# New margins and key offsets in the planner of an attention and mixture-of-experts kernel

## The chip, the cores and the metric

The kernel runs on one core of one Trainium2 chip. The metric is the device time of one execution in microseconds. Three runs of the kernel before gave 558.15, 562.72 and 568.16 us; their median, 562.72 us, is the time that a change is held against.

## The reference, cut to what matters

Linear attention without a softmax feeds a mixture of experts with top-1 routing. The shapes: 8 batches ("blocks" below), 8 heads, 576 rows, 64 columns per head, so 4608 tokens of 512 columns; 8 experts with a hidden width of 1024; a capacity of 1152 tokens per expert. All inputs are fp32.

```python
kv = np.einsum('bhsd,bhse->bhde', k, v)
out = np.einsum('bhsd,bhde->bhse', q, kv)
rms = np.sqrt(np.mean(out * out, axis=-1, keepdims=True) + 1e-06)
x = (out / rms * g_norm)                      # then (B, H, S, D) -> (B*S, H*D)
...
logits = x @ w_gate
expert_idx = np.argmax(logits, axis=1)        # gate_w: its softmax probability
...
h = np.maximum(np.einsum('ecd,edf->ecf', disp, w1), 0.0)   # disp: an expert's tokens, in order
y = np.einsum('ecf,efd->ecd', h, w2)
out[i] = gate_w[i] * y[expert_idx[i], pos[i]]
```

## The kernel before

The work has two stages, each with a plan of its own.

**Attention stage** (first plan, some 155 us with the first expert's beginning). For each of the 8 blocks, `load` (L736) fetches k, v and q in halves of four heads. `kv_products` (L758) makes k-transposed times v for each half: one run of 36 products of 64 columns, in TensorE's rows `a<-v_sb,k_sb` and `misc<-v_sb,k_sb` of L772 in turn. These are the "k and v runs". Their sums are copied (`kvs`), transposed (L801), copied again (`kvt`), multiplied with the gate's weights (the gate product, L810) and spread into a block-diagonal right-hand side, `kv_bd`. `unit` (L829) transposes q (L843, four transposes or one), copies (`qt`) and multiplies with `kv_bd` (the attention products, L861, or L864 for half rows) into `o_sb`, which also gets the gate's logits.

`route` (L905) does the top-1 routing of a block, mostly on VectorE: sums of squares (`ss`, L894), the root, logits, the winner's one-hot `ohe`. Then come two products on TensorE, both with key FIRST, the most urgent. `place` (L995, matmuls of L1003, "first routing product") counts each token's position within its expert; VectorE turns the positions into one-hots (`ohl` L1032, `ohh` L1035, `rhs` L1039). `enter` (L1044, matmuls of L1046, "second routing product") adds the tokens to a table. The results, rows with logits, go to DRAM (`x_dram`).

After block 2 the largest expert so far is picked (`early_weights`, L1166): its weights are loaded in quarters into `raw`, VectorE takes maxima of eight pieces (`top`, L361, tile `am`), and a scale follows through two small products (L374, L381) and six short steps of VectorE. After block 4 the first 384 tokens of that expert are gathered (`early_slots` L1208, `rows` L1230: an indirect DMA, a scaling `norm` L465 into `xm`, four transposes L477, the "turning", a high half L713 and a low half L485 of `xs`) and its products begin while the last blocks still run.

**Expert stage** (second plan). For each of 8 experts, products with w1 (L551, three terms of fp16 halves), a ReLU into high and low halves `hb` (L556 on ScalarE, L559 on VectorE), products with w2 (`second`, L1262; L597, or L612 and L627 for narrow tiles), an eviction with a scale (`ysb`, L632 on ScalarE) and a scattering DMA (L637). Weights of the next expert are split (`weights`, L1611) and its rows gathered (`rows_beside`, L1663) beside that.

**What sets the order.** `Plan` (L111) is a list scheduler that runs while the kernel is built. Every `op` has ways (engine and assumed duration), dependences, a key and a margin `late`. An op may start when its dependences have ended, plus a lag between the engines, plus `late` (L145). The planner takes, over all engines, the op that can start soonest; among those of an engine that could start then, the lowest key wins. `NUDGE` holds two tables, one for each plan, that add an offset to the key of single ops by their number. The resulting order is emitted as it is, engine by engine. The margins only steer this order; on the chip nobody waits for a margin.

In the kernel before, the margins are 1.9 us for the second run of a block's k and v products (`KV_APART`, L64 and L778), `LANDED` (3.0) for rows of the later experts, and those of two small products. `place`, `enter`, the maxima and the first gathered rows have none.

```python
return op(("T", KV), go, [ts["k", half][1], ts["v", half][1]] + mm, key + (0, 0.8)[half], banks, (kh, vh),
          late=KV_APART if half and b else 0.0)
```

Of the kernel before, what the change touches and what calls it, by code (L numbers as in the profile page):

```python
# [12 lines left out]
F32 = mybir.dt.float32  # L13
I32 = mybir.dt.int32
AF = mybir.ActivationFunctionType
ALU = mybir.AluOpType
# [5 lines left out]
EARLY_AFTER = 4  # L22
# [24 lines left out]
FIRST = -50.0  # L47
# [25 lines left out]
GATHER = 1.2  # L73
LANDED = 3.0
TURNED_PAIR = {64: 2.7, 48: 2.2, 32: 1.8}
NUDGE = (
# [10 lines left out]

# [102 lines left out]
def attention_moe_kernel(  # L190
# [12 lines left out]
    nc = tc.nc  # L203
    NB, H, S, D = q.shape
    N, DM = out.shape
    E = w_gate.shape[1]
    F = w1.shape[2]
    P = 128
# [225 lines left out]
    def spans(s0, s1):  # L434

        cuts = [s0] + list(range((s0 // P + 1) * P, s1, P)) + [s1]
        return [(a, b - a, NHI if a % P else a // P) for a, b in zip(cuts, cuts[1:])]
# [89 lines left out]
    class Gemm1:  # L527
# [14 lines left out]
        def out(self, t, j):  # L542
            return t[:, j, 0:self.n].rearrange("p (u x) -> p u x", u=self.nh)
# [29 lines left out]
    class Gemm2:  # L573
# [50 lines left out]
        def turn(self, i, yp):  # L624
            n = self.tiles[i][1]
            for dt in range(KD):
                nc.tensor.transpose(yp[0:n, dt * P:(dt + 1) * P], self.yt[:, dt * n:(dt + 1) * n], ident)  # L627

        def out(self, i, yp):
            n = self.tiles[i][1]  # L630
            self.ysb = self.pool.tile([P, DM], F32, tag="ysb", name="ysb", bufs=self.bufs)
            nc.scalar.activation(self.ysb[0:n], yp[0:n, 0:DM], AF.Copy, scale=self.ysc[0:n, i:i + 1])  # L632
            return self.ysb
# [71 lines left out]
    op = plan.op  # L705
# [199 lines left out]
    def route(b, oh, ssh, outs, sums):  # L905
# [99 lines left out]

        bp = op(("T", 0.4), place, [ohe] + accs[-1:] + reads[-1:], FIRST)
        acc = V(0.08, lambda: nc.vector.tensor_tensor(out=tot_acc, in0=tot_acc, in1=z["oh_sum"], op=ALU.add),
# [43 lines left out]
        o2 = V(0.45, low_hot, [lo], takes=(lh,))  # L1051
        ent = op(("T", 0.21), enter, [o, o2] + enters[-1:] + readers.pop("tab", []), FIRST, (), (rh, lh))
        enters.append(ent)
# [112 lines left out]
    def early_weights():  # L1166
# [11 lines left out]
        for i, key in ((0, W1_KEY), (1, W2_KEY)):  # L1178
# [6 lines left out]
            for p in range(4):  # L1185
                key = WKEYS[i][0] + 2 * p * WKEYS[i][1]
                if TOPS[i][p] == "A":
                    tops += [op(("A", 0.8), lambda e, f=f, p=p: f["sum"](p), [loads[p // 2]], key)
                             for p in (2 * p, 2 * p + 1)]
                else:  # L1190
                    tops += [op(("V", 0.61), lambda e, f=f, p=p: f["top"](p), [loads[p // 2]], key)
                             for p in (2 * p, 2 * p + 1)]
# [37 lines left out]
    def rows(gidx, s0, s1, n, slots_, key, low, pool, raw, bank, hold=None, size=None):  # L1230
# [10 lines left out]
        for i in range(len(spans(s0, s1))):  # L1241
# [4 lines left out]
            a = op([("V", 0.61), ("P", 1.05)], lambda e, i=i: st["rows"].norm(i, nc.vector if e == "V" else nc.gpsimd), [o],  # L1246
                   low, (xm,), (xg,), port="VP")
            gates.append(op(("V", 0.07), lambda e, i=i: st["rows"].gate(i), [o], low, (), (xg, hold)))

# [12 lines left out]
    def second(r, st, hh, hl, w2, scaled, hid, w_hold, sl_hold, s0, s1, bank, tiles=range(NHI), key=None):  # L1262
# [3 lines left out]
        for i, (_, m, _) in enumerate(spans(s0, s1)):  # L1266
# [37 lines left out]

            o = op(("A", 0.58), out_, [o], urgent, (yh,), (yp,))
            o = op(("P", 1.05), lambda e, i=i, yh=yh: st["g2"].write(i, yh.t), [o], key, (), (yh, sl_hold))
            o = op(("D", 0.73), None, [o], key, (), (yh,))
# [303 lines left out]
    def weights(r, key, after, after2):  # L1611

        ws, sets, zs, holds = wsets[r % 2], [], [], []
        for i in range(2):
# [19 lines left out]
            for p in range(8):  # L1634
                if MOE_TOPS[i][p] == "A":
                    tops.append(op(("A", 0.8), lambda e, f=f, p=p: f["sum"](p), [loads[p // 2]], key, (hold,),
                                   (raws[p // 2],)))
                else:
                    tops.append(op(("V", 0.61), lambda e, f=f, p=p: f["top"](p), [loads[p // 2]], key, (),
                                   (raws[p // 2],)))  # L1640
            x = new("x")
# [21 lines left out]
    def rows_beside(r, key):  # L1663
# [9 lines left out]
        for i in range(n):  # L1673
            xg, xm, pair = new("xg"), new("xm"), new("pair")

            def fetch(e, i=i):
                if i == 0:
# [9 lines left out]
                   lambda e, i=i: st["x"].norm(i, by_letter[e]), [o], key - 5 if r == 1 else key + 1,  # L1687
                   (xm,), (xg,), late=0.0 if r == 1 else LANDED, port="VP")
            gates.append(op(("P", 0.25), lambda e, i=i: st["x"].gate(i, nc.gpsimd), [a], key + 1, (), (xg, hold)))
# [120 lines left out]
```

## Time and profile before

| | |
|---|---|
| median of three runs | 562.72 us (558.15 to 568.16) |
| profiled execution | 556.98 us, span 555.1 us |
| mean granted clock of TensorE | 0.985 |
| TensorE busy | 520.3 us, 94% of the span |
| VectorE busy | 394.1 us, 71% |
| ScalarE busy | 252.7 us, 46% |
| GpSimd busy | 150.9 us, 27% |

The engines are named PE (TensorE's matmuls), PEld (its weight loads), DVE (VectorE), ACT (ScalarE), POOL (GpSimd) and SP (the queue that issues most loads). Matmuls overlap in a pipeline, so the start of the next row tells more of a matmul's length than its own duration does. "Issue" marks idle time for which the profile shows nothing that was waited for.

### The profile page before, as it was taken

The page shows a single profiled execution, that of the slowest core. Times are in us where ns is not written, and L with a number is a line of the kernel's source. Part 1 is how long each engine was busy: PE and PEld are TensorE (multiplying, and loading weights), DVE is VectorE, ACT ScalarE, POOL GpSimd, SP SyncE. Part 2 cuts the span into 40 slices and gives each one's busy share as a digit, 9 for nine tenths or more (in the row PEclk, how much of TensorE's full clock was granted, in tenths as well). Part 3 has the DMA queues.
Part 4 walks back from the last instruction along what each step waited for, and adds up shares of the span by engine and source line. Part 5 has one row for each costly group of instructions (what it writes and reads, how often), then busy time and mean ns, then how long its engine had stood idle before and what let it go on. Part 6 is the DMA issues. An engine that isn't in the chain of part 4 may idle for free.

```text
span 555.1 us, 12017 instructions
## 1 busy us (share of the span) xinstructions
PE 520.3 (94%) x4599; PEld 344.2 (62%) x4599; DVE 394.1 (71%) x1041; ACT 252.7 (46%) x506; POOL 150.9 (27%) x173
## 2 busy tenths in 40 slices
PE   4989797898996999999999999999999999999995
PEld 4878695876544666546754675667468648745442
DVE  3389679989967679869868899779778785751200
ACT  1667475698413346237246282264246165212210
POOL 6001002612356553243404320220503151002011
PEclk9999798899999999999999999999999999999998
DMA  8999999744256979778619538747529341001010
GB/s 272 358 356 360 392 380 368 252 144 182 98 155 249 226 242 264 154 151 266 159 49 322 144 92 280 139 144 259 142 65 305 115 119 38 1 20 58 0 40 32
DMA packets 78019, 102.58 MB, mean 185 GB/s; under 512 B 43222, under 2 KB 51414, under 8 KB 76932
## 3 DMA queue, kind: packets, MB, share of 16 engines
q1 hardware_dynamic: 69600, 70.43, 43.3%
q0 software_dynamic: 7776, 31.30, 16.0%
q8 instruction: 38, 0.62, 0.5%
q14 instruction: 25, 0.20, 0.1%
q10 hardware_dynamic: 580, 0.02, 0.1%
HBM read 73.13 MB, written 20.61 MB: 169 GB/s over the span
## 4 chain that ended last, share of the span: by engine, by line
PE 19%; issue 18%; DMA 11%; DVE 3%; POOL 1%; ACT 1%; POOLq 0%; DVEq 0%
DMA out_dram<-ysb,si 11%; PE hp L551 11%; PE yp L597 6%; DVE am L361 2%; PE yp L612 1%; ACT w2h L395 1%; POOL xg L457 1%; DVE hb L559 1%; POOL out_dram L637 0%; POOL gt L472 0%; POOLq L1740 0%; POOLq L637 0%; DVE xm L465 0%; ACT hb L556 0%; DVE w2l L401 0%
## 5 line engine op out<-in xcount | busy, mean ns | idle before, releaser
L551 PE MATMUL hp<-xs,w1h 128*128 128x320 f16 (+6 forms) x896 | 134.6, 300 | 5.7 <-ACT xs L713 2.6
L597 PEld LDWEIGHTS <-hb 128*128 128x128 f16 x840 | 81.2, 98 | 93.4 <-issue 0.7
L597 PE MATMUL yp<-w2h,hb 128*128 128x512 f16 x544 | 127.1, 379 | 0.3 <-ACT ysb L632 0.2
L551 PEld LDWEIGHTS <-w1h 128*128 128x128 f16 x960 | 93.3, 98 | 46.9 <-issue 7.8
L637 POOL DMA_INDIRECT out_dram<-ysb,si x41 | 46.3, 1130 | 238.1 <-ACT ysb L632 180.8
L361 DVE TENSOR_REDUCE am<-raw 128x1 f32<-128x512 f32 x120 | 75.3, 677 | 12.5 <-DMA raw<-in_moe_w_dram 12.4
L556 ACT ACTIVATE hb<-hp 128x320 f16<-128x320 f32 (+7 forms) x64 | 40.6, 636 | 84.8 <-PE hp L551 70.9
L559 DVE SCALAR_TENSOR_TENSOR hb<-hp,hb 128x320 f16<-128x320 f32 (+7 forms) x64 | 47.2, 737 | 35.8 <-ACT hb L556 35.6
L551 PE MATMUL hp<-xs,w1l 128*128 128x320 f16 (+6 forms) x448 | 71.5, 300 | 0.0
L632 ACT ACTIVATE ysb<-yp,ysc 128x512 f32<-128x512 f32 (+5 forms) x40 | 27.4, 684 | 94.2 <-PE yp L597 90.9
L597 PE MATMUL yp<-w2l,hb 128*128 128x512 f16 x272 | 64.7, 379 | 0.0
L551 PEld LDWEIGHTS <-w1l 128*128 128x128 f16 x480 | 46.9, 98 | 19.4
L457 POOL DMA_INDIRECT xg<-x_dram,gi x35 | 37.1, 1061 | 34.5 <-DVE xm L465 19.8
L861 PE MATMUL op<-kv_bd,qt 128*128 128x144 f32 x256 | 44.2, 316 | 1.6 <-ACT qt L713 1.1
L401 DVE SCALAR_TENSOR_TENSOR w2l<-raw,sw,w2h 128x512 f16<-128x512 f32 x64 | 44.8, 743 | 0.5 <-ACT w2h L395 0.4
L401 DVE SCALAR_TENSOR_TENSOR w1l<-raw,sg,w1h 128x512 f16<-128x512 f32 x64 | 45.0, 746 | 0.0
L491 ACT CAST pair<-xm 128x512 f16<-128x512 f32 (+5 forms) x35 | 21.3, 615 | 46.1 <-DVE xm L465 24.1
L395 ACT ACTIVATE w1h<-raw,sg 128x512 f16<-128x512 f32 x60 | 38.8, 711 | 7.0 <-DVE sg L390 7.0
L395 ACT ACTIVATE w2h<-raw,sw 128x512 f16<-128x512 f32 x62 | 40.1, 713 | 1.0 <-DVE sw L331 1.0
L861 PEld LDWEIGHTS op<-kv_bd,qt 128*128 128x128 f32 x256 | 37.8, 210 | 3.8 <-ACT qt L713 1.8
L772 PE MATMUL a<-v_sb,k_sb 64*64 64x64 f32 x576 | 23.6, 233 | 9.2 <-DMA v_sb<-in_v_dram 7.4
L772 PEld LDWEIGHTS a<-v_sb,k_sb 64*64 64x64 f32 x576 | 20.7, 145 | 12.9 <-issue 11.6
(250 smaller groups left out, 634.6 us busy)
## 6 DMA issues: line engine op xcount, KB each, us to landing
raw<-in_moe_w_dram SPq DMA_DIRECT2D x64, 512.0 KB
k_sb<-in_k_dram SPq DMA_DIRECT2D x16, 576.0 KB
v_sb<-in_v_dram SPq DMA_DIRECT2D x16, 576.0 KB
x_dram<-o_sb POOLq DMA_DIRECT2D x8, 1152.0 KB
q_sb<-in_q_dram SPq DMA_DIRECT2D x16, 512.0 KB
x_dram<-o_sb POOLq DMA_DIRECT2D x8, 144.0 KB
q_sb<-in_q_dram SPq DMA_DIRECT2D x32, 32.0 KB
out_dram<-ysb,si POOLq DMA_INDIRECT x41
```

The source lines that it names most:

```text
L361: nc.vector.tensor_reduce(out=am()[:, p:p + 1], in_=raw[:, sl(p)], axis=AX.X, op=ALU.max, apply_absolute_value=True)
L395: nc.scalar.activation(wh[:, sl(p)], raw[:, sl(p)], AF.Copy, scale=z["s"])
L401: nc.vector.scalar_tensor_tensor(out=wl[:, sl(p)], in0=raw[:, sl(p)], scalar=z["s"], in1=wh[:, sl(p)], op0=ALU.mult, op1=ALU.subtract)
L457: nc.gpsimd.indirect_dma_start(out=self.xg[i][0:n], out_offset=None, in_=x_dram[0:self.rows, :], in_offset=bass.IndirectOffsetOnAxis(ap=se ...
L551: nc.tensor.matmul(self.view(hp)[:, u], lhsT=w[:, c, j * P:(j + 1) * P], rhs=x[:, c, u * hw:(u + 1) * hw], start=(t == 0 and c == 0), stop ...
L556: nc.scalar.activation(self.out(self.hh, j), self.view(hp), AF.Relu)
L559: nc.vector.scalar_tensor_tensor(out=self.out(self.hl, j), in0=self.view(hp), scalar=0.0, in1=self.out(self.hh, j), op0=ALU.max, op1=ALU.s ...
L597: nc.tensor.matmul(yp[0:n, 0:DM], lhsT=h[:, j, o:o + n], rhs=w[:, j, :], start=(m == 0), stop=(m == len(self.terms) - 1))
L632: nc.scalar.activation(self.ysb[0:n], yp[0:n, 0:DM], AF.Copy, scale=self.ysc[0:n, i:i + 1])
L637: nc.gpsimd.indirect_dma_start(out=out[:, :], out_offset=bass.IndirectOffsetOnAxis(ap=self.sidx[0:n, col:col + 1], axis=0), in_=ysb[0:n], ...
L772: nc.tensor.matmul(banks[g].t[rows[u], half * D:(half + 1) * D], lhsT=kh.t[rows[g], u, c * D:(c + 1) * D], rhs=vh.t[rows[g], u, c * D:(c + ...
L861: nc.tensor.matmul(y, lhsT=qt.t[:, i * P:(i + 1) * P], rhs=kv2[:, half * HH + i], start=True, stop=True)
```

## The change

Five things are altered. (1) `norm` and `gate` of the first gathered rows, and `norm` of the second expert's, get a margin of 1.5 us (`ROWS_LAND`). (2) The weight maxima get 1.3 us (`LOADS_LAND`): those of the first expert on either engine, those of the later ones on VectorE. (3) `place` gets 1.0 us and `enter` 1.5 us, but 0.4 and 0.5 us in blocks 4 and 7. (4) The very last eviction is cut into two halves of 256 columns, one on ScalarE and one on VectorE. (5) Both tables of `NUDGE` are replaced. The line of the k and v runs, `KV_APART` with its use, is the same in both kernels.

```diff
+ROWS_LAND = 1.5
+LOADS_LAND = 1.3
+PLACE_LATE = (1.0, 0.4)
+ENTER_LATE = (1.5, 0.5)
 NUDGE = (
-    {79: 1.6, 93: 2.6, 148: 0.4, 162: -1, 176: 1.8, 184: -8.3, 187: -5.1, 188: 10.3, 220: 0.3, 229: -4, 267:
+    {9: -3, 23: -0.1, 67: 3, 75: 3.9, 82: 2.5, 154: 0.5, 220: 2.7, 229: -1.5, 269: 1.3, 293: 3.6, 301: -0.7,
...
+        def out_half(self, i, yp, ysb, half, eng):
+            n = self.tiles[i][1]
+            c = slice(half * DM // 2, (half + 1) * DM // 2)
+            if eng == "A":
+                nc.scalar.activation(ysb[0:n, c], yp[0:n, c], AF.Copy, scale=self.ysc[0:n, i:i + 1])
+            else:
+                nc.vector.tensor_scalar(out=ysb[0:n, c], in0=yp[0:n, c], scalar1=self.ysc[0:n, i:i + 1], scalar2=None,
+                                        op0=ALU.mult)
...
-        bp = op(("T", 0.4), place, [ohe] + accs[-1:] + reads[-1:], FIRST)
+        soon = b in (EARLY_AFTER, NB - 1)
+        bp = op(("T", 0.4), place, [ohe] + accs[-1:] + reads[-1:], FIRST, late=PLACE_LATE[soon])
...
-        ent = op(("T", 0.21), enter, [o, o2] + enters[-1:] + readers.pop("tab", []), FIRST, (), (rh, lh))
+        ent = op(("T", 0.21), enter, [o, o2] + enters[-1:] + readers.pop("tab", []), FIRST, (), (rh, lh),
+                 late=ENTER_LATE[soon])
...
-                    tops += [op(("V", 0.61), lambda e, f=f, p=p: f["top"](p), [loads[p // 2]], key)
+                    tops += [op(("V", 0.61), lambda e, f=f, p=p: f["top"](p), [loads[p // 2]], key, late=LOADS_LAND)
...
-                   low, (xm,), (xg,), port="VP")
-            gates.append(op(("V", 0.07), lambda e, i=i: st["rows"].gate(i), [o], low, (), (xg, hold)))
+                   low, (xm,), (xg,), late=ROWS_LAND, port="VP")
+            gates.append(op(("V", 0.07), lambda e, i=i: st["rows"].gate(i), [o], low, (), (xg, hold), late=ROWS_LAND))
...
+            if r == E - 1 and i == len(spans(s0, s1)) - 1:
+                o = [op((e, 0.33), lambda e, f=half_, h=h: f(e, half=h), [o], urgent, (yh,), (yp,)) for h, e in enumerate("AV")]
+            else:
+                o = [op(("A", 0.58), out_, [o], urgent, (yh,), (yp,))]
...
-                                   (raws[p // 2],)))
+                                   (raws[p // 2],), late=LOADS_LAND))
...
-                   (xm,), (xg,), late=0.0 if r == 1 else LANDED, port="VP")
+                   (xm,), (xg,), late=ROWS_LAND if r == 1 else LANDED, port="VP")
```

The order before and after is shown at three places of TensorE. In the changed kernel the lines of these rows are higher by about 20 (L772 is L791 there, L843 is L862, L861 is L880, L864 is L883, L801 is L820, L810 is L829, L1003 is L1022, L1046 is L1066, L381 is L388, L1086 is L1107).

The first place is the two k and v runs of the fifth block (block 4, buffers 192 and 186). Before, the end of the first and the start of the second:

```order
L772 MATMUL a<-v_sb_192,k_sb_191 64x64
L772 MATMUL misc<-v_sb_192,k_sb_191 64x64
L843 MATMUL qp<-ident,q_sb_187 128x128
L772 MATMUL a<-v_sb_186,k_sb_185 64x64
L772 MATMUL misc<-v_sb_186,k_sb_185 64x64
```

Now, from the end of the second block's `enter`, which follows the first run directly, to the start of the second run:

```order
L1066 LDWEIGHTS ohl
L1066 MATMUL tab<-rhs,ohl 128x96
L862 MATMUL qp<-ident,q_sb_190 128x128 x4
L862 MATMUL qp<-ident,q_sb_187 128x128
L862 MATMUL qp<-ident,q_sb_190 128x128 x4
L880 MATMUL op<-kv_bd_135,qt 128x144 x4
L791 MATMUL a<-v_sb_186,k_sb_185 64x64
L791 MATMUL misc<-v_sb_186,k_sb_185 64x64
```

One transpose stood between the two runs; now the second block's `enter`, nine transposes and two attention products do.

The second place is the fourth block (block 3) between `place` and `enter`. Before:

```order
L1003 LDWEIGHTS upto_97
L1003 MATMUL misc<-ohe,upto_97 128x8
L843 MATMUL qp<-ident,q_sb_190 128x128 x4
L861 MATMUL op<-kv_bd_135,qt 128x144 x4
L843 MATMUL qp<-ident,q_sb_190 128x128 x5
L1046 LDWEIGHTS ohl
L1046 MATMUL tab<-rhs,ohl 128x96
```

Now, from the end of `place` to the k and v run, behind whose 36 products five transposes and then `enter` stand:

```order
L1022 LDWEIGHTS upto_97
L1022 MATMUL misc<-ohe,upto_97 128x8
L829 MATMUL a<-wgs,kvt 128x32 x2
L883 MATMUL op<-kv_bd_133,qt 64x144 x2
L862 MATMUL qp<-ident,q_sb_190 128x128 x8
L880 MATMUL op<-kv_bd_135,qt 128x144 x4
L791 MATMUL a<-v_sb_186,k_sb_185 64x64
L791 MATMUL misc<-v_sb_186,k_sb_185 64x64
```

What stood between the two routing products was three rows; a k and v run and two more rows have moved in between.

The third place is the fifth block (block 4) between `place` and `enter`. Before, behind the block's `place` and four transposes:

```order
L381 MATMUL misc<-bm,ones_bf 128x1
L801 MATMUL a<-ident,kvs 128x128 x2
L1086 LDWEIGHTS ones_93
L1086 MATMUL misc<-tot_acc,ones_93 128x8
L861 MATMUL op<-kv_bd_135,qt 128x144 x4
L843 MATMUL qp<-ident,q_sb_193 128x128 x4
L861 MATMUL op<-kv_bd_135,qt 128x144 x4
L810 MATMUL a<-wgs,kvt 128x32 x2
L861 MATMUL op<-kv_bd_135,qt 128x144 x2
L1046 LDWEIGHTS ohl
L1046 MATMUL tab<-rhs,ohl 128x96
```

Now, from the end of `place`:

```order
L1022 MATMUL misc<-ohe,upto_97 128x8
L883 MATMUL op<-kv_bd_135,qt 64x144 x2
L388 LDWEIGHTS ones_bf
L388 MATMUL misc<-bm,ones_bf 128x1
L820 MATMUL a<-ident,kvs 128x128 x2
L1107 LDWEIGHTS ones_93
L1107 MATMUL misc<-tot_acc,ones_93 128x8
L862 MATMUL qp<-ident,q_sb_187 128x128 x4
L829 MATMUL a<-wgs,kvt 128x32 x2
L862 MATMUL qp<-ident,q_sb_187 128x128 x4
L1066 LDWEIGHTS ohl
L1066 MATMUL tab<-rhs,ohl 128x96
```

The five attention products of L861 have left the gap between the two routing products; one half-row product and four more transposes have come in.

## Rows read from the trace of the kernel before

**Rows 1.** The page's first part: busy us, share of the span, instructions of each engine.

```profile
PE 520.3 (94%) x4599; PEld 344.2 (62%) x4599; DVE 394.1 (71%) x1041; ACT 252.7 (46%) x506; POOL 150.9 (27%) x173
```

**Rows 2.** Stretches of 20 us: length, busy us (instructions) per engine, PEclk, DMA share, GB/s.

```profile
60.00:80.00 20.00, 16.99 (x246) 15.39 (x239) 11.29 (x43) 11.65 (x31) 1.13 (x2) 0.83 1.05 383
80.00:100.00 20.00, 16.01 (x242) 13.66 (x241) 19.01 (x79) 12.23 (x34) 5.90 (x8) 0.86 1.06 377
340.00:360.00 20.00, 20.00 (x171) 12.19 (x170) 15.80 (x29) 4.93 (x8) 4.96 (x8) 1.00 0.86 217
```

**Rows 3.** TensorE's waits: who waited for whom, us in total, times, longest.

```profile
PE tab L1046 <- DVE rhs L1039: 2.7, 2, 2.5
PE hp L551 <- ACT xs L713: 2.6, 1, 2.6
PE misc L1003 <- issue: 2.5, 1, 2.5
PE a L772 <- issue: 1.7, 3, 0.9
PE x L477 <- DVE xs L485: 1.4, 1, 1.4
```

**Rows 4.** The same view as rows 2, around two idle stretches and two low clocks.

```profile
60.80:63.45 2.65, 0.13 (x6) 0.06 (x2) 0.04 (x1) 0.00 (x0) 1.13 (x2) 1.00 1.04 375
63.59:70.41 6.82, 6.63 (x30) 6.32 (x30) 4.25 (x22) 4.40 (x13) 0.00 (x0) 0.50 1.05 395
89.35:91.90 2.55, 0.06 (x2) 0.14 (x2) 2.55 (x10) 0.56 (x2) 0.73 (x1) 1.00 1.06 367
94.31:101.13 6.82, 6.53 (x36) 5.75 (x37) 5.92 (x30) 3.95 (x9) 3.94 (x4) 0.50 0.97 370
```

**Rows 5.** TensorE's time line, 63 to 103 us: start, us, line, operation, tiles, idle before.

```profile
63.40 0.18 PE L1003 MATMUL misc<-ohe,upto 128*128 128x8 f16 x1 [2.52 <-issue]
...
83.55 1.33 PE L864 MATMUL op<-kv_bd,qt 128*64 128x144 f32 x8
...
86.21 0.22 PE L1003 MATMUL misc<-ohe,upto 128*128 128x24 f16 x3
...
87.60 1.25 PE L861 MATMUL op<-kv_bd,qt 128*128 128x144 f32 x8 [0.68 <-ACT qt L713]
88.68 0.71 PE L843 MATMUL qp<-ident,q_sb 128*128 128x128 f32 x5
91.88 0.71 PE L1046 MATMUL tab<-rhs,ohl 128*128 128x96 f16 x5 [2.49 <-DVE rhs L1039]
...
102.49 0.71 PE L1046 MATMUL tab<-rhs,ohl 128*128 128x96 f16 x5
```

**Rows 6.** VectorE's time line, 87 to 92 us.

```profile
87.51 0.67 DVE L894 TENSOR_REDUCE ss<-sq 128x8 f32<-128x512 f32 x1
88.10 0.18 DVE L1016 TENSOR_REDUCE pos_all<-inc 128x5 int32<-128x40 f32 x1
...
90.19 1.27 DVE L361 TENSOR_REDUCE am<-raw 128x1 f32<-128x512 f32 x2
91.38 0.45 DVE L1039 TENSOR_TENSOR rhs<-ohh,tok_hl 128x480 f16<-128x480 f16 x1
```

**Rows 7.** The view of rows 2, instructions of L772 alone, over the fifth block's two runs.

```profile
57.30:60.05 2.75, 2.49 (x144) 2.28 (x144) 1.00 1.02 395
```

**Rows 8.** VectorE's time line, 95 to 99 us.

```profile
95.96 0.15 DVE L1007 TENSOR_TENSOR tot_acc<-tot_acc,oh_sum 128x8 f16<-128x8 f16 x1
...
98.15 0.19 DVE L1016 TENSOR_REDUCE pos_all<-inc 128x5 int32<-128x40 f32 x1
```

**Rows 9.** The page's third part: a DMA queue's packets, MB, share of 16 engines.

```profile
q8 instruction: 38, 0.62, 0.5%
```

**Rows 10.** ScalarE's time line, at the hand-over and at the end.

```profile
169.62 0.86 ACT L713 CAST xs<-xp 128x512 f16<-128x512 f32 x2 [5.24 <-remote]
...
548.51 0.69 ACT L632 ACTIVATE ysb<-yp,ysc 128x512 f32<-128x512 f32 x1 [4.49 <-PE yp L597]
```

More of the change, by code (lines that the diff above doesn't have):

```diff
@@ L627, in turn, with out_tile @@
                 nc.tensor.transpose(yp[0:n, dt * P:(dt + 1) * P], self.yt[:, dt * n:(dt + 1) * n], ident)
+        def out_half(self, i, yp, ysb, half, eng):
[6 more added lines that the diff above has]
+                                        op0=ALU.mult)
+        def out_tile(self):
+            return self.pool.tile([P, DM], F32, tag="ysb", name="ysb", bufs=self.bufs)
         def out(self, i, yp):
             n = self.tiles[i][1]
-            self.ysb = self.pool.tile([P, DM], F32, tag="ysb", name="ysb", bufs=self.bufs)
+            self.ysb = self.out_tile()
             nc.scalar.activation(self.ysb[0:n], yp[0:n, 0:DM], AF.Copy, scale=self.ysc[0:n, i:i + 1])
@@ L1187, in early_weights @@
                 if TOPS[i][p] == "A":
-                    tops += [op(("A", 0.8), lambda e, f=f, p=p: f["sum"](p), [loads[p // 2]], key)
+                    tops += [op(("A", 0.8), lambda e, f=f, p=p: f["sum"](p), [loads[p // 2]], key, late=LOADS_LAND)
                              for p in (2 * p, 2 * p + 1)]
                 else:
-                    tops += [op(("V", 0.61), lambda e, f=f, p=p: f["top"](p), [loads[p // 2]], key)
+                    tops += [op(("V", 0.61), lambda e, f=f, p=p: f["top"](p), [loads[p // 2]], key, late=LOADS_LAND)
                              for p in (2 * p, 2 * p + 1)]
@@ L1303, in out_, with half_ @@
                 yh.t = st["g2"].out(i, yp.t)
-            o = op(("A", 0.58), out_, [o], urgent, (yh,), (yp,))
-            o = op(("P", 1.05), lambda e, i=i, yh=yh: st["g2"].write(i, yh.t), [o], key, (), (yh, sl_hold))
+            def half_(e, i=i, yp=yp, yh=yh, half=0):
+                yh.t = yh.t or st["g2"].out_tile()
+                st["g2"].out_half(i, yp.t, yh.t, half, e)
+            if r == E - 1 and i == len(spans(s0, s1)) - 1:
+                o = [op((e, 0.33), lambda e, f=half_, h=h: f(e, half=h), [o], urgent, (yh,), (yp,)) for h, e in enumerate("AV")]
+            else:
+                o = [op(("A", 0.58), out_, [o], urgent, (yh,), (yp,))]
+            o = op(("P", 1.05), lambda e, i=i, yh=yh: st["g2"].write(i, yh.t), o, key, (), (yh, sl_hold))
             o = op(("D", 0.73), None, [o], key, (), (yh,))
```

21 rows, old and new, of the table NUDGE are left out of this document.

## The prediction

> **What bounds the kernel now.** I read the page's first part, then the busy time in stretches of 20 us, then TensorE's waits, then time lines where the longest waits stand. TensorE is busy 94% of the span, the next engine, VectorE, 71% (its 394.1 us stand in the same row) [rows 1]. By stretches the two stages part [rows 2]: in the expert stage TensorE fills its stretches (20.00 of 20 us at 340), and an order can give nothing back there. In the attention stage it doesn't: 16.99 and 16.01 us of 20 at 60 and 80 us. VectorE is close behind, 19.01 of 20 at 80 us, but only 11.29 at 60 us, so what TensorE loses at 60 us VectorE loses too. The sum is therefore made of single waits of the attention stage and of the hand-over to the second plan.
>
> Those waits [rows 3]: 2.7 us for VectorE's `rhs` (2.5 of it in one wait), 2.6 us for ScalarE's `xs`, 2.5 us marked "issue" inside a first routing product, 1.4 us before the turned rows. Two of them cost twice. 0.2 us behind the end of the 2.5 us hole, and 2.4 us behind the end of the wait for `rhs`, the granted clock is 0.50, the lower of its two levels, for 6.82 us each; in the idle stretches themselves it was still 1.00 [rows 4]. TensorE is busy for 6.63 and 6.53 us there, with work that takes half as long at the upper level: 3.3 us are lost each time.
>
> The profiled execution took 556.98 us, 1.9 us of it around the span of 555.1. The median of the runs shown, 562.72, lies 5.7 us above it; I carry the change of the profiled execution over to the median.
>
> **The change, part by part.** No work is added: the counts per engine stay, but for one eviction cut in two and a handful of copies that change between VectorE and ScalarE. What changes is where things stand.
>
> *Second routing product of the fourth block (ENTER_LATE 1.5).* Before, TensorE had three rows between the block's two routing products: four transposes, two attention products, five transposes. It was done with them at 91.88 - 2.49 = 89.39 us and waited, since VectorE had a sum of squares (0.67 us) and three weight maxima (a pair took 1.27) ahead of `rhs` [rows 5, 6]. Now a gate product, a half-row product, eight transposes, two attention products, a whole k and v run and five transposes stand between them: 0.6 + 0.63 + 1.1 + 1.08 + 1.25 + 0.7 = 5.4 us (0.63 is half of the 1.26 us from 83.55 to the run at 84.81; 1.08 us is 87.60 to 88.68; a transpose is 0.14 us by the 0.71 us of five; the gate product is put at the half-row product's; the run is half of the 2.49 us of rows 7). VectorE still has two sums of squares and three maxima to do in between; from place to the end of `rhs` it took 86.43 to 91.83, 5.4 us. Little is left to wait, some 0.3 us. **Gain 2.2 us**, between 0 (if a weight's transfer holds the maxima) and 2.5.
>
> *The same product of the fifth block (ENTER_LATE 0.5 there).* This goes the other way. Before, five attention products stood between its two routing products, and TensorE, on its lower clock, found `rhs` ready at 102.49 us without a wait [rows 5]. Now a half-row product, the second small product of the weights' scale, two transposes of k-v, a count, eight transposes and a gate product are left: 0.63 + 0.1 + 0.3 + 0.1 + 1.1 + 0.6 = 2.8 us. VectorE's chain still holds the six short steps of the weights' scale, 2.19 us from the update of the totals to the positions [rows 8]; from the positions to the end of `rhs` the fourth block took 88.10 to 91.83, 3.73 us, less 0.67 for one maximum and 1.27 for a pair, so 1.8 at most [rows 6]; a sum of squares (0.67) stands ahead. 4.0 to 4.7 us together. **Loss 1.8 us**, between 0 and the 2.5 of the fourth block's wait before. The sixth block's attention products are queued behind it on TensorE, and VectorE's table and the gather follow it.
>
> *The k and v runs.* The change is named for a rule that keeps them apart, but that rule (KV_APART, a delay of 1.9 us) stands in both kernels word for word. The order obeys it better all the same. For the fifth block a single transpose stood between the two runs, 144 short matmuls in 2.75 us, 2.49 of them busy [rows 7]; 0.8 us behind them TensorE stood for 2.52 us with no releaser shown, in the middle of the third block's routing product, whose operands were there [rows 4, 5]. Now a routing product, nine transposes and two attention products part the runs. I read the hole as the instruction stream running dry behind so many short instructions, and take it as gone: **gain 2.5 us**, between 0 and 2.5; and with it the low clock that follows, **gain 3.3 us**, between 0 and 3.3. The other fall of the clock I leave as it is, since the fifth block's wait comes in place of the fourth's: 0, down to a gain of 3.3.
>
> The Trainium skill speaks against this term: its page "Runtime: NRT & Kernel Launch", section "Instruction fetch mechanics", has instructions come in blocks of 16 KiB while the block before is executed, so that crossing into a new one is mostly hidden. The size agrees with the queue's row, 0.62 MB in 38 packets [rows 9]; that it is hidden is what the trace doesn't bear out where a hole has no releaser. By that rule both gains come to nothing, which is a rival below.
>
> *Gathered rows (ROWS_LAND).* For the first expert's first rows the third turning now comes sooner behind the second, and the first product stands right behind it. What the 1.4 us wait of rows 3 gives back I take as lost there: 0, within 1.4 either way. At the hand-over to the second plan TensorE waited 2.6 us for `xs`, and ScalarE had stood 5.24 us before that cast with a releaser that the profile doesn't tell [rows 10], so the plan alone doesn't explain it. Now eight products stand before the last turning and none behind it, and ScalarE has an eviction (0.69 us) that becomes due with the turning, ahead of the last cast (0.43, half of the 0.86 us of two) [rows 10]; with 0.4 us for two hand-overs between engines some 1.5 us. **Gain 1.1 us**, between 0 and 2.6.
>
> *Weight loads (LOADS_LAND).* At the hand-over VectorE's order has six maxima ahead of the expert's first low half, as before: 0.
>
> *Second block.* Its first attention product now follows the gate product directly, where eight transposes stood. **Loss 0.2 us**, up to 1.1, the eight transposes.
>
> *Last eviction in halves.* 0.69 us on ScalarE at the very end [rows 10] become two halves side by side on ScalarE and VectorE, which has nothing else left. **Gain 0.3 us**, between 0 and 0.35.
>
> Sum: -2.2 + 1.8 - 2.5 - 3.3 - 1.1 + 0.2 - 0.3 = -7.4 us: 549.6 for the profiled execution, **555.3 us** for the median.
>
> **Rivals.** *The hole comes back.* Nothing in the planner prices instructions, and the k and v runs keep their length; other runs show holes too, 1.7 us in three [rows 3]. Against it: the longest hole stands behind the closest pair. Then 2.5 and 3.3 fall away, -1.6 us is left: 561.1. The rule of the Trainium skill's page gives the same.
>
> *Both falls go.* If the fifth block's wait stays clearly below the 2.5 us of the two that the low clock followed, TensorE keeps its upper level through the stage: -7.4 - 3.3 = -10.7, and -12.5 if VectorE, fed earlier, hides that wait as well: 550.2. For it speak VectorE's 8.7 us of idle time at 60 us, against it its 19.01 of 20 at 80 us [rows 2].
>
> *Slower: the fifth block's wait starts a fall of its own.* Its place is that block's second routing product, where TensorE has nothing else to turn to. If a maximum waits for its weights there, the wait passes 2.5 us and the clock falls behind it, while the fall behind the fourth block stays (something else late there) and the hole is back: -1.6 + 0.7 + 3.3 = +2.4 us: 565.1. It decides from a wait of about 2.5 us.
>
> **Chances.** Forecast 0.42 (its own range 551 to 560); the hole comes back 0.28; both falls go 0.20; slower 0.10. The bounds of the costs, with the 10 us by which the three runs shown differ, give 547 to 567. About 2%, 11.3 us, is what a measurement of this kernel can tell from no change. Faster by more (below 551.5) takes most of the third case and a tail of the first: 0.20. Slower by more (above 574) lies past even the slower rival: 0.05. Within: 0.75.
>
> **What would show it.** Right: no wait above 1 us at the fourth block's second routing product; one of about 2 us at the fifth's; no "issue" hole above 1 us within 2 us of a pair of k and v runs; one stretch of clock 0.50 after the first 30 us and before 130 us instead of two; about 1.5 us before the second plan's first expert product; ScalarE's last eviction at half its length. Wrong: TensorE idle by more than a few us in the expert stage; two or more falls of the clock; holes that move to other runs; a wait that is new and above 2 us, wherever it stands.

## The result and the profile after

The changed kernel took 567.15 us (median of four runs, 565.85 to 569.48), the kernel before beside it 561.34 (558.15 to 568.16): a ratio of 1.0117, 95% interval 1.0072 to 1.0161. The ratios, here and below, are taken over the runs within 1.5% of the fastest of each kernel, so they are not the quotients of the medians. Run again on two chips (e3 and e13 below) the changed kernel gave 1.0103 [1.0065, 1.0141] and 1.0111 [1.0069, 1.0153]. So it is slower by about 1.1%, 6 us, where 555.3 was forecast; 567.15 lies just past the end of the range. The profiled execution took 567.97 us, its span is 566.1.

The page's first part (columns as in [rows 1]):

```profile
PE 516.6 (91%) x4599; PEld 340.6 (60%) x4599; DVE 396.9 (70%) x1036; ACT 252.5 (45%) x510; POOL 148.9 (26%) x175
```

TensorE has no more work than before (520.3 us there), only more idle time. The view by stretches, first two of [rows 2], then the 60 us around the hand-over:

```profile
60.00:80.00 20.00, 16.07 (x249) 14.36 (x249) 13.50 (x51) 11.94 (x32) 1.46 (x3) 0.91 1.04 340
...
340.00:360.00 20.00, 20.00 (x125) 12.04 (x123) 19.00 (x33) 6.38 (x10) 1.00 (x1) 1.00 0.54 197
160.00:180.00 20.00, 16.50 (x89) 9.24 (x88) 11.74 (x37) 4.31 (x8) 9.72 (x11) 0.91 0.79 279
180.00:200.00 20.00, 16.70 (x94) 9.56 (x93) 12.60 (x28) 5.29 (x12) 11.42 (x14) 0.91 0.54 148
200.00:220.00 20.00, 17.33 (x148) 11.39 (x147) 14.58 (x32) 13.52 (x22) 10.17 (x9) 0.91 0.62 212
```

The kernel before, in the last two of these stretches, not shown ahead of the prediction:

```profile
180.00:200.00 20.00, 19.84 (x163) 11.96 (x161) 15.31 (x32) 10.18 (x18) 11.22 (x12) 1.00 0.85 196
200.00:220.00 20.00, 19.49 (x137) 13.17 (x136) 16.96 (x37) 10.76 (x18) 7.57 (x9) 1.00 0.92 286
```

From 180 to 220 us TensorE lost 5.3 us of busy time against before, and a clock of 1.00 became 0.91. This is the beginning of the expert stage, of which the prediction had said that an order can give nothing back there. TensorE's waits, as in [rows 3]:

```profile
...
PE op L880 <- ACT qt L732: 5.5, 5, 3.5
PE hp L558 <- DVE hb L566: 4.7, 2, 3.3
PE qp L862 <- DMA q_sb<-in_q_dram: 3.8, 2, 3.4
PE yp L634 <- DVE yt L626: 2.7, 1, 2.7
PE hp L558 <- ACT xs L732: 2.5, 1, 2.5
...
PE tab L1066 <- DVE rhs L1059: 2.1, 2, 1.9
```

The 2.5 us "issue" hole is gone, the wait for `xs` is as long as it was, and the long waits for `qt`, `hb` and `yt` are new. (`yt` is VectorE's sum of the narrow tile's products, which TensorE transposes before the eviction; `p2t`, below, is a short step of a weights' scale, behind the maxima.) TensorE's time line, at the steps that the prediction named (compare [rows 5]) and behind the hand-over:

```profile
62.73 1.20 PE L862 MATMUL qp<-ident,q_sb 128*128 128x128 f32 x5 [3.42 <-DMA q_sb<-in_q_dram]
...
90.00 0.71 PE L1066 MATMUL tab<-rhs,ohl 128*128 128x96 f16 x5 [0.22 <-DVE rhs L1059]
...
104.02 0.71 PE L1066 MATMUL tab<-rhs,ohl 128*128 128x96 f16 x5 [1.91 <-DVE rhs L1059]
112.32 1.25 PE L880 MATMUL op<-kv_bd,qt 128*128 128x144 f32 x8 [3.48 <-ACT qt L732]
...
172.55 3.76 PE L558 MATMUL hp<-xs,w1h 128*128 128x320 f16 x16 [2.46 <-ACT xs L732]
178.44 1.25 PE L558 MATMUL hp<-xs,w1h 128*128 128x320 f16 x8 [1.04 <-DVE p2t L336]
185.16 1.77 PE L558 MATMUL hp<-xs,w1h 128*128 128x320 f16 x8 [3.30 <-DVE hb L566]
209.80 1.06 PE L634 MATMUL yp<-ident,yt 128*64 128x128 f32 x4 [2.67 <-DVE yt L626]
```

The last two have a low clock behind them, one of them here in the view of [rows 4]; it costs about 1.7 us (3.41 us at half speed):

```profile
185.73:189.14 3.41, 3.41 (x15) 1.91 (x14) 2.10 (x6) 0.44 (x1) 1.62 (x3) 0.50 1.04 343
```

A third such stretch begins in the wait for `xs`; the first trace of the kernel before has none at its hand-over.

### The profile page after: what moved, and what is told of

Read it like the earlier page. It is cut to its first block, busy times and chain, and to the rows that moved or that the text cites. A ratio compares the mean times of both kernels' runs of the same rounds, so it can differ in the third digit from the quotient of the medians.

```text
span 566.1 us, 12006 instructions
## 1 busy us (share of the span) xinstructions
PE 516.6 (91%) x4599; PEld 340.6 (60%) x4599; DVE 396.9 (70%) x1036; ACT 252.5 (45%) x510; POOL 148.9 (26%) x175
## 4 chain that ended last, share of the span: by engine, by line
PE 35%; issue 22%; DMA 21%; DVE 11%; ACT 4%; POOL 3%; another core or an unknown queue 1%; POOLq 0%; SPq 0%; DVEq 0%; ACTq 0%
PE hp L558 13%; DMA out_dram<-ysb,si 12%; PE yp L604 9%; DMA q_sb<-in_q_dram 5%; PE op L880 3%; DVE am L368 3%; PE op L558 3%; DMA v_sb<-in_v_dram 2%; POOL xg L464 2%; DMA raw<-in_moe_w_dram 1%; PE qp L862 1%; DVE hb L566 1%; ACT w1h L402 1%; PE yp L619 1%
## 5 line engine op out<-in xcount | busy, mean ns | idle before, releaser
L558 PE MATMUL hp<-xs,w1h 128*128 128x320 f16 (+6 forms) x896 | 137.5, 305 | 8.2 <-DVE hb L566 4.7
L558 PEld LDWEIGHTS <-w1h 128*128 128x128 f16 x960 | 95.0, 99 | 50.4 <-issue 9.9
L464 POOL DMA_INDIRECT xg<-x_dram,gi x35 | 39.2, 1121 | 39.5 <-DVE xm L472 31.2
L880 PE MATMUL op<-kv_bd,qt 128*128 128x144 f32 x256 | 42.6, 308 | 6.9 <-ACT qt L732 5.5
L408 DVE SCALAR_TENSOR_TENSOR w1l<-raw,sg,w1h 128x512 f16<-128x512 f32 x64 | 47.2, 778 | 2.1 <-ACT w1h L402 2.1
L880 PEld LDWEIGHTS op<-kv_bd,qt 128*128 128x128 f32 x256 | 36.5, 204 | 9.4 <-ACT qt L732 6.5
L791 PE MATMUL a<-v_sb,k_sb 64*64 64x64 f32 x576 | 22.1, 230 | 11.6 <-DMA v_sb<-in_v_dram 10.1
L913 DVE TENSOR_REDUCE ss<-sq 128x8 f32<-128x512 f32 x40 | 26.8, 676 | 6.3 <-ACT sq L908 5.9
L862 PE MATMUL qp<-ident,q_sb 128*128 128x128 f32 x144 | 23.8, 289 | 7.4 <-DMA q_sb<-in_q_dram 3.8
```

The costliest lines, as they stand in the source:

```text
L408: nc.vector.scalar_tensor_tensor(out=wl[:, sl(p)], in0=raw[:, sl(p)], scalar=z["s"], in1=wh[:, sl(p)], op0=ALU.mult, op1=ALU.subtract)
L464: nc.gpsimd.indirect_dma_start(out=self.xg[i][0:n], out_offset=None, in_=x_dram[0:self.rows, :], in_offset=bass.IndirectOffsetOnAxis(ap=se ...
L558: nc.tensor.matmul(self.view(hp)[:, u], lhsT=w[:, c, j * P:(j + 1) * P], rhs=x[:, c, u * hw:(u + 1) * hw], start=(t == 0 and c == 0), stop ...
L862: nc.tensor.transpose(qp.t[:, i * P:(i + 1) * P], x[:, at_:at_ + P], ident)
L880: nc.tensor.matmul(y, lhsT=qt.t[:, i * P:(i + 1) * P], rhs=kv2[:, half * HH + i], start=True, stop=True)
L913: nc.vector.tensor_reduce(out=ss[:, col], in_=sq.t, axis=AX.X, op=ALU.add)
```

## The experiments

Five of the eighteen kernels take a plan's order whole (e1 to e4, e13); in the others single steps are moved in it by hand. For that, `emit` takes an order that is written out:

```diff
-    def emit(self):
-        for o in self.place():
+    def emit(self, order=None):
+        ops = self.place()
+        if order:
+            ...
+            ops = [self.ops[int(x[:-1])] for x in order.split()]
+        for o in ops:
```

The runs were made on four chips (e1 to e8, e9 to e12, e13 to e16, e17 and e18). Each ratio is against the kernel before on the same chip, with its 95% interval.

### Which plan, and what repeats (e1 to e4)

e1 is the kernel before with the changed kernel's order of the first plan, e2 the changed kernel with the old order of the first plan:

```diff
-    plan.emit()
+    plan.emit(ORDERS[0])
...
-    plan.emit()
+    plan.emit(ORDERS[1])
```

> The kernel before, with the order of the changed kernel forced on the first plan alone (attention stage and the first expert's beginning); the second plan keeps its old order. Theory A (the loss is made by the second plan's new order, in the first 40 us behind the hand-over): the time stays within 2 us of before, between 559 and 563 us beside a before of 561, and the stretch from 170 us behind the start to 215 us has at most 3 us of idle TensorE and no more than one fall of the clock. Theory B (the attention stage's new waits and the first loads that landed 2.4 us later carry it): 5 to 7 us slower than before, as the whole change.

> The changed kernel with the old order forced on the first plan; the second plan has the new order and the last eviction is in halves. Theory A: 5 to 7 us slower than before, with TensorE waits of together 6 us or more and two or three falls of the clock in the first 45 us behind the hand-over. Theory B: within 2 us of before.

> The changed kernel once more, without an edit, for a second trace and for its time beside the others. Both theories: about 1.012 of before. If the waits of the first trace belong to the order, the same ones come again (3.3 us for hb at the second expert product group, 2.7 us for yt, three falls of the clock between 170 and 215 us); if they were chance, they stand elsewhere, and the first matmul starts at 6.4 us again.

> The kernel before once more, without an edit, for a second trace. If the waits of the first trace belong to the order: the 2.5 us hole behind the pair of k and v runs and the 2.5 us wait for rhs come again, the first matmul at 6.4 us. If they were chance, they stand elsewhere.

Measured: e1 1.0034 [0.9998, 1.0070], e2 1.0082 [1.0051, 1.0112], e3 1.0103. The second plan carries most of it, and its three waits (`p2t` or maxima, `hb`, `yt`) come again in e2 and e3. e4's span was 564.2 us, 9 us above the first trace of the same kernel: it has a wait of 4.0 us for `hb` at 271 us that the first trace has not, and e1, with the same second plan, has it too (3.9). So single traces differ by as much as the whole effect, and I read only what repeats.

### Three moves that failed (e5 to e8)

In e5 a load goes back on SP's queue: the new order has the second half of v first, so that the first product waits for three loads.

```diff
-v, second half
 k, first half
 v, first half
 k, second half
+v, second half
```

> The changed kernel with one load moved: the second half of the first block's v goes back from the first to the fourth place of SP's queue, so that the first half's k and v are again the first two loads; nothing else moves. Theory A (three loads now have to land before the first product instead of two, and the whole program starts later by that): first matmul at 6.4 us instead of 8.0 to 8.8, time 2 us below the changed kernel's (about 1.008 of before, where the changed kernel has 1.0103). Rival (the first product is late for another reason, or the time is caught up before the hand-over): no difference of the time, and the first expert's first product stays at 131 to 136 us.

Measured: first matmul at 6.43 us as expected (it stood at 7.7 to 8.8 in the twelve other traces with the new first order, 6.35 to 6.61 with the old), but 1.0109 [1.0077, 1.0141]: no gain. The late start is real and costs nothing that can be measured.

In e6 VectorE's `xm` goes behind the next two low halves, in e7 GpSimd's three gathers behind two scatters, in e8 both, with e5's load:

```diff
-xm, third rows                       (VectorE)
 hb, third low half
 hb, fourth low half
+xm, third rows
...
-xg, three gathers                    (GpSimd)
 out_dram, scatter
 out_dram, scatter
+xg, three gathers
```

> The changed kernel with one step moved on VectorE: the scaling of the second expert's third rows (xm) stands behind the fourth low half hb instead of ahead of the third; everything else in order. Theory A (xm waits for its buffer and holds hb, hb holds TensorE, and the clock falls behind it): the wait of 2.0 to 3.3 us for hb about 10 us behind the hand-over goes, with one fall of the clock (1.7 us): 3 to 5 us below the changed kernel. Rival (VectorE waits there for what comes late anyway): the same wait stands one step later, at the next hb, no gain.

> The changed kernel with three gathers of the third expert's rows moved on GpSimd's queue behind the next two scatters, so that they no longer run while TensorE ends the first expert's narrow tile. Theory A (the 2.6 us wait for yt, seen in all three traces with this order to end 0.6 to 0.7 us after the third gather's issue, comes from that row of gathers): the wait shrinks below 1 us and the fall of the clock behind it goes: 2 to 4 us below the changed kernel. Rival (VectorE and ScalarE wait there for TensorE's own end): the wait stays at 2.6 us wherever the gathers stand, no gain.

> The changed kernel with all three moves at once: the load back, xm later, the gathers later. Theory A: the gains add up to 7 to 11 us, which puts it 1 to 5 us below the kernel before (0.990 to 1.000 of it), with at most one fall of the clock between the hand-over and 45 us behind it. Rival: the waits move to other places and the sum stays above the kernel before (1.005 or more).

Measured: e6 1.0088 [1.0055, 1.0121] with the same 3.3 us wait for `hb`: `xm` was late with everything else and not the cause. e7 1.0184, e8 1.0234: the wait for `yt` was gone in both, as expected, and a larger one came. GpSimd's and TensorE's time lines in e7:

```profile
202.24 1.02 POOL L786 DMA_INDIRECT out_dram<-ysb,si  x1 [3.65 <-ACT ysb L781]
210.83 0.93 POOL L786 DMA_INDIRECT out_dram<-ysb,si  x1 [7.57 <-DMA out_dram<-ysb,si]
212.07 1.00 POOL L594 DMA_INDIRECT xg<-x_dram,gi  x1 [0.30 <-issue]
```

```profile
219.45 2.96 PE L688 MATMUL hp<-xs,w1h 128*128 128x336 f16 x10 [7.29 <-DVE hb L696]
```

The second scatter waits 7.57 us for the first one to land, the gathers stand behind it, and VectorE's `xm` and `hb` behind the gathers. That is the mechanism, found in the wrong place: two scatters stand next to each other at the hand-over of the changed kernel as well.

### Two scatters next to each other (e9 to e12)

GpSimd in the changed kernel at the hand-over:

```profile
170.26 1.01 POOL L656 DMA_INDIRECT out_dram<-ysb,si  x1 [0.30 <-ACT ysb L651]
178.90 0.99 POOL L656 DMA_INDIRECT out_dram<-ysb,si  x1 [7.63 <-DVE y L338]
...
182.53 1.06 POOL L472 TENSOR_TENSOR xm<-xg 128x512 f32<-128x512 f32 x1
```

ScalarE behind that `xm`, then VectorE:

```profile
183.62 0.62 ACT L498 CAST pair<-xm 128x512 f16<-128x512 f32 x1 [5.75 <-POOL xm L472]
184.15 0.76 ACT L563 ACTIVATE hb<-hp 128x320 f16<-128x320 f32 x2
```

```profile
184.61 0.49 DVE L566 SCALAR_TENSOR_TENSOR hb<-hp,hb 128x320 f16<-128x320 f32 x1 [0.46 <-ACT hb L563]
```

GpSimd stands for 7.63 us (the profile puts it down to a small step of VectorE that merely ended last; e7 and e12 name the scatter's transfer), `xm` comes at 182.53, ScalarE's `pair` and `hb` behind it, VectorE's `hb`, and TensorE starts at 185.16. Before, two gathers and a scaling stood between the two scatters, and the second had 3.09 us to wait:

```profile
164.82 1.12 POOL L637 DMA_INDIRECT out_dram<-ysb,si  x1 [0.30 <-issue]
...
173.82 1.03 POOL L637 DMA_INDIRECT out_dram<-ysb,si  x1 [3.09 <-ACT hb L556]
```

e9 moves the second scatter, e10 puts the three later gathers behind one scatter only, e11 does both and takes the copy `next_i` ahead of a gather, and e12 makes the pair in the kernel before:

```diff
 out_dram, scatter                    (e9)
-out_dram, scatter
 gt, xg, pair, xm, gt, xg, pair
+out_dram, scatter
...
-out_dram, scatter                    (e12)
 xg, xg, xm
+out_dram, scatter
 out_dram, scatter
```

> The changed kernel with one scatter moved on GpSimd's queue: the second of two that stand directly behind each other at the hand-over goes behind the next pair of low halves, scalings and gathers. Theory A2 (the second scatter waits about 7.6 us for the first to land, holds GpSimd's queue with the second expert's scaling xm, xm holds ScalarE's pair and the high half hb behind it, and that holds TensorE): GpSimd's idle time before that scatter goes below 3 us, TensorE's wait of 1.5 to 3.3 us for hb about 12 us behind the hand-over goes with the fall of the clock behind it, 3 to 5 us below the changed kernel (1.002 to 1.006 of before). Rival (what is late there is the weights' transfer): the wait stays, 1.009 or more.

> The changed kernel with the three gathers moved behind the next scatter only, so that they stand between two scatters and no longer run while the first expert's narrow tile ends. Theory A2 (these gathers cause the 2.6 us wait for yt; behind both scatters they were too late because the second scatter waits for the first): the wait for yt stays away as in the run before, and the 7.3 us wait for hb that came in its place shrinks to 2 us or less: 1 to 4 us below the changed kernel. Rival (any later gather is too late): a wait for hb above 3 us some 50 us behind the hand-over, no gain.

> The changed kernel with both of these moves and a third: the copy that names the second expert, for which its weight loads wait, goes back ahead of the gathers, so that these loads are issued 1.3 us earlier. Theory A2: waits of 1.0 to 3.0 us for the weight maxima shrink as well; the sum of TensorE's idle time in the 45 us behind the hand-over falls from 7 us to 3 us or less: 5 to 9 us below the changed kernel, 0.993 to 1.002 of before. Rival: 1.005 or more, since other waits take their place.

> The kernel before with one scatter moved: the first of the two goes behind two gathers and a scaling, directly ahead of the second, as the changed kernel has them. Theory A2: GpSimd stands about 7 us at the second, TensorE waits 2 to 3 us more for hb some 10 us behind the hand-over, and the clock falls once more: 3 to 5 us slower than before (1.005 to 1.009). Rival (the two scatters cost nothing): within 1 us of before, 0.998 to 1.002.

Measured: e9 1.0004 [0.9972, 1.0036], e10 1.0151 [1.0104, 1.0199], e11 1.0031 [0.9999, 1.0062], e12 1.0038 [1.0013, 1.0063]. e9's second scatter waits 0.25 us and no wait for `hb` above 1 us is left within 45 us of the hand-over. e12 has the chain that the theory says, with a wait of TensorE of 3.0 us at its end; GpSimd's part of it:

```profile
167.97 1.03 POOL L767 DMA_INDIRECT out_dram<-ysb,si  x1 [0.20 <-issue]
175.15 0.99 POOL L767 DMA_INDIRECT out_dram<-ysb,si  x1 [6.16 <-DMA out_dram<-ysb,si]
```

It costs 2.1 us there, less than the 3 to 5 expected. e10 and e11 say that all three gathers are too late behind a scatter: in e11 VectorE waits 4.57 us for one.

### On one chip (e13 to e16)

e9's chip lacked the wait for `yt` even with the gathers in their place, so e13 to e16 put the changed kernel beside the moved ones. e15 is e9 with the copy `next_i`, for which the second expert's weight loads wait on SP, ahead of one gather:

```diff
 xg<-x_dram,gi_rest, three gathers
+next_i<-perm_i
 xg<-x_dram,gi
-next_i<-perm_i
```

> The changed kernel without an edit, on the same chip as the next three. Theory A2 (the two scatters next to each other carry the loss): 1.008 to 1.013 of before, GpSimd idle for more than 7 us ahead of the second scatter, TensorE waiting 1.5 to 3.3 us for hb behind it. Rival (the late signals of TensorE carry it, which come on some chips alone): where the trace shows none of these, within 1.004 of before in spite of GpSimd's idle time.

> The changed kernel with the second scatter moved, as in e9, beside the changed kernel itself on one chip. Theory A2: 3 to 6 us below e13, 0.998 to 1.005 of before. Rival: within 1.5 us of e13.

> e14, and the copy that names the second expert goes back ahead of the gathers, without moving the three later gathers. Theory A2: the waits for the weight maxima behind the hand-over (2.3 us in e9) shrink below 1 us: 1 to 3 us below e14, 0.994 to 1.001 of before. Rival (the weight loads land no sooner, the queue is full): no difference from e14.

> e15 with the kernel before's order in the first plan. If the first plan's new order costs the 0.3% that it showed alone: 1 to 3 us below e15, 0.990 to 0.998 of before, faster than both kernels. Rival (the two orders of the first plan are worth the same): the same as e15.

Measured: e13 1.0111, e14 1.0044 [1.0004, 1.0085], e15 0.9994 [0.9955, 1.0033], e16 1.0006 [0.9972, 1.0039]. With a before of 560.85 us the scatter is worth 3.8 us and the copy 2.8 us. Each is known to some 3 us, so the copy's part by itself isn't clear of the noise; the two together, 6.6 us, are, and with both the loss is gone. Between the first plan's two orders no difference can be told (e15 and e16), to some 3 us. Waits of TensorE from 160 to 215 us in e13, e14 and e15:

```profile
PE hp L558 <- DVE p2t L336: 3.0, 1, 3.0
PE yp L634 <- DVE yt L626: 2.7, 1, 2.7
PE hp L558 <- DVE hb L566: 2.0, 1, 2.0
PE hp L558 <- ACT xs L732: 1.7, 1, 1.7
```

```profile
PE yp L764 <- DVE yt L756: 2.7, 1, 2.7
PE hp L688 <- DVE p2t L466: 1.9, 1, 1.9
PE hp L688 <- ACT xs L862: 1.8, 1, 1.8
```

```profile
PE yp L764 <- DVE yt L756: 2.7, 1, 2.7
PE hp L688 <- ACT xs L862: 2.4, 1, 2.4
PE hp L688 <- DVE p2t L466: 0.5, 1, 0.5
PE hp L688 <- DVE hb L696: 0.5, 1, 0.5
```

The wait for `hb` goes with the scatter (0.5 us stands in e15). The one for `p2t`, which stands behind the maxima of the weights, shrinks from 3.0 to 1.9 us with the scatter and to 0.5 with the copy: the loads are issued 4.8 us ahead of the second plan's first product in e14, 7.0 us in e15, as in the kernel before (7.4).

### One gather fewer in the row (e17, e18)

What was left is the 2.7 us for `yt`. In e17, e15's order, the last of the three gathers goes behind the next scatter:

```diff
 xg, two gathers
-xg, third gather
 out_dram, scatter
+xg, third gather
```

> e15 (scatter moved, copy of the second expert's name moved) and one more move: the last of the row of three gathers goes behind the next scatter, the two that are needed first stay. If the row's length sets the wait for yt: it shrinks from 2.7 to about 1.4 us, and the time is 1 to 3 us below e15 (0.993 to 0.998 of before). Rival (it is one gather or the scatter before that delays TensorE's signal): the wait stays at 2.7 us; or the moved gather comes too late and a wait for hb above 2 us stands 50 us behind the hand-over, 1.000 or more. On a chip without late signals neither shows and the time is that of e15.

> e17 with the kernel before's order in the first plan. If the first plan's two orders are worth the same, as e15 and e16 had it, within 1.5 us of e17; if the new one costs 0.3%, 2 us below it. Faster than the kernel before if e17 gains: 0.992 to 0.998.

Measured: e17 **0.9952 [0.9921, 0.9983]**, e18 0.9981 [0.9947, 1.0014]. The wait is 1.27 and 1.23 us, one gather less, as expected. TensorE in e17:

```profile
204.40 0.63 PE L764 MATMUL yp<-ident,yt 128*64 128x128 f32 x4 [1.27 <-DVE yt L756]
```

e17 is the changed kernel with three steps of GpSimd's queue moved. It lies 0.5% below the kernel before on its chip, clear of its interval; e18, with the same second plan, isn't clear of it. Neither e15 nor the changed kernel ran on that chip, so what the last move gave in time isn't shown; what its trace shows is the shorter wait.

## Why the prediction was wrong

*Expert stage: the step that failed.* "In the expert stage TensorE fills its stretches (20.00 of 20 us at 340), and an order can give nothing back there." The stretch at 340 us stood for the whole stage; the 45 us behind the hand-over have no such fill, and there I read VectorE's maxima and ScalarE's casts but never GpSimd's order. On it two scatters had come together (3.8 us by e13 and e14) and a copy had gone behind a gather (2.8 us by e14 and e15, not clear of noise alone). The first is a dependence that the planner doesn't know: it counts a scatter's transfer as 0.73 us, and no step as waiting for it but the release of a buffer; at the hand-over and in e7 the next scatter stands for 6.2 to 7.7 us from the end of the issue. The copy is one that it does know (the weight loads have it among their dependences), so there its durations let the copy go back; which of them is wrong isn't shown. The Trainium skill, "DMA: Bandwidth & Descriptors", section "Anatomy of one DMA — SWDGE (gpsimd) path", says that a semaphore is waited for on the issuing sequencer, so that GpSimd itself stands; the trace agrees, with everything behind the scatter late. The same section's fit, about 2.0 us and the bytes at 436 GB/s, makes 2.6 us for the tile's 0.26 MB, an estimate. Late in the kernel before the trace agrees:

```profile
502.81 0.97 POOL L637 DMA_INDIRECT out_dram<-ysb,si  x1 [2.49 <-DMA out_dram<-ysb,si]
```

At the hand-over of the changed kernel it doesn't, with 7.63 us; there the DMA engines moved 405 GB/s (171.27 to 178.90 us), here 89 GB/s (500 to 506 us). That this load makes the difference is likely and not shown.

*Weight loads: 0 forecast, some 2.8 us lost.* "VectorE's order has six maxima ahead of the expert's first low half, as before" is true; what changed is when their weights were asked for.

*Fourth block's `enter`: right.* 2.49 us became 0.22 (0.3 forecast). *Fifth block's: right.* 1.91 us, where 1.8 was forecast, and 1.91 or 1.92 in the thirteen other traces of the new first order; a wait of 0.8 us just ahead of it was not forecast.

*The hole and the low clock: wrong, 5.8 us.* The hole did go: it stands in all six traces of the old first order (1.7 to 2.5 us, "issue") and in none of the new. But TensorE waits there for q's load instead, 2.0 to 3.5 us in each of the fourteen (in two of them some 12 us later). The step that failed is the one that asks what is late next: I named nothing. That the hole was the instruction stream running dry is not shown. Nor did the low clock go: in the attention stage it cost 6.5 us on the mean of the six old traces and 7.1 on that of the fourteen new (half the length of the stretches), behind other waits. The longest of these in the changed kernel's trace, 3.48 us for `qt` at the sixth block's attention products, stands in no sum of mine; in the thirteen other new traces it is 0.7 to 2.9 us. Nor does the clock fall from a wait of about 2.5 us on, as two rivals had it: behind 2.67 us for `yt` it fell in the changed kernel, behind 2.7 us in e14 and e15 it stayed at 1.00. So the fourth block's gain is paid back at the fifth, the rest never came, and the first expert's first product stands at 133.0 us on the mean of the old (131.2 to 135.3) and 133.7 of the new (129.5 to 138.5): nothing gained of the 6.0 forecast for this stage.

*Hand-over: wrong.* 1.1 us were to go; 2.46 stand where 2.56 stood. I had seen that ScalarE's releaser was not told [rows 10] and had still costed it by the plan. The runs show what it may be, below: on e9's chip TensorE waits at most 0.7 us for this `xs` in all four traces, in the sixteen others 1.6 to 2.6 us.

*Last eviction: wrong in sign.* The halves were taken as side by side. ScalarE, VectorE and the scatter in the changed kernel:

```profile
559.42 0.47 ACT L640 ACTIVATE ysb<-yp,ysc 128x256 f32<-128x256 f32 x1 [4.49 <-PE yp L604]
```

```profile
559.92 0.48 DVE L642 TENSOR_SCALAR ysb<-yp,ysc 128x256 f32<-128x256 f32 x1 [19.95 <-ACT ysb L640]
```

```profile
560.68 0.97 POOL L656 DMA_INDIRECT out_dram<-ysb,si  x1 [4.52 <-DVE ysb L642]
```

VectorE's half waits for ScalarE's. Both write one tile (`ysb`) and read one (`yp`); which of the two parts them isn't shown. From the first half to the scatter 1.26 us, where the whole eviction took 0.96 (548.51 to 549.47 in the first trace): 0.3 us lost instead of won.

Of the rivals, "the hole comes back" had the right size for the first plan, by another mechanism; the slower one had the wrong place. Its own place, the fifth block, behaved as forecast.

*Still open.* Why the late start costs nothing; what the hole is; and the first plan's share, 0.3% in e1, none between e15 and e16, reversed between e17 and e18.

## What to carry to other kernels

An order has to be read on every queue, and on the one that issues transfers first of all: a store that must wait for the store before it holds everything behind it, however idle its engine looks (26% busy here). Put between two dependent transfers the work that the others wait for, and give a planner the time at which the second one can be issued. A stage that is full on the mean has a beginning that isn't; read that stretch by itself before a cost of nothing is written down for it.

## What the runs showed of the hardware

On three of the four chips of the experiments TensorE's signals came late while GpSimd issued a row of gathers. In the changed kernel the products that `yt` and `ysb` wait for had begun by 205.99 us, the last of them 1.03 us long, and VectorE and ScalarE both got on at 209.05 and 209.11:

```profile
207.41 0.95 POOL L464 DMA_INDIRECT xg<-x_dram,gi  x1 [0.30 <-issue]
```

```profile
209.05 0.69 DVE L626 TENSOR_REDUCE yt<-yp 128x256 f32<-128x512 f32 x1 [3.43 <-remote]
```

```profile
209.11 0.69 ACT L651 ACTIVATE ysb<-yp,ysc 128x512 f32<-128x512 f32 x1 [3.71 <-remote]
```

That is 0.7 us behind the end of the third gather's issue (208.36). The wait was gone when the gathers were moved away (e7, e8), and shrank by one gather when one left the row (e17, e18). ScalarE's 5.24 us at the hand-over [rows 10] ended in the same way, 1.1 us behind the last gather's issue (168.48). So did the wait for `qt` in the attention stage, 1.2 us behind the second of three gathers, though the four transposes it needs had begun by 108.18 us and take 0.66:

```profile
109.52 1.00 POOL L464 DMA_INDIRECT xg<-x_dram,gi_first  x1 [0.31 <-issue]
```

```profile
111.68 0.58 ACT L732 COPY qt<-qp 128x512 f32<-128x512 f32 x1 [3.93 <-remote]
```

On e9's chip the wait for `yt` didn't come: the same order of products and the same three gathers (the last at 199.87 us),

```profile
198.66 0.69 DVE L756 TENSOR_REDUCE yt<-yp 128x256 f32<-128x512 f32 x1 [0.57 <-PE yp L749]
```

so the chip seems to decide on 2.6 us, and with it on a fall of the clock, which stands behind six of the nine waits of 2.6 to 2.7 us for `yt`. This order was traced once on that chip; its four short waits for `xs` at the hand-over point the same way. How a row of gathers delays a signal of TensorE no run here shows.
